# Regrouping the front of a one-core attention and MLP kernel: four max and six projection products in turn, the first maxima turned in four squares, four lead products moved behind exponential ones

## The chip, the core and the metric

The kernel runs on one core of a Trainium2 chip. The core has a matrix engine (PE, with a weight-load side PEld), a vector engine (DVE), a scalar engine (ACT), GpSimd (POOL) and a queue engine (SP) that issues transfers. PE writes into PSUM, eight banks of 128 partitions x 512 float32 numbers; DVE and ACT read them from there. The metric is device time in microseconds (us), lower is better. The kernel before took 1555.54 us, the median of three runs (1554.82 to 1555.70).

## The reference

A block of a transformer with modulated norms, 2048 rows of width 512, 32 query heads of width 16 over a single key and value head, and an MLP of width 1376:

```python
mod = (_silu(c) @ w_mod).reshape(c.shape[0], 6, 1, -1)
sa, ca, ga, sb, cb, gb = (mod[:, i] for i in range(6))
h = _layernorm(x) * (1 + ca) + sa
q, k, v = (h @ wq), h @ wk, h @ wv            # q: 32 heads of 16
p = _softmax(einsum("bhqd,bkd->bhqk", q, k) * 16 ** -0.5)
x = x + ga * (einsum("bhqk,bkd->bhqd", p, v) @ wo)
h = _layernorm(x) * (1 + cb) + sb
x = x + gb * (_gelu(h @ w1 + b1) @ w2 + b2)
```

The softmax subtracts each row's maximum, so every score is needed twice: once for the maximum, once for the exponential.

## The kernel before

**Units.** The attention is cut into 64 units: 8 blocks of 256 rows times 8 groups of four heads. For a unit there are 32 *max products* (`m`, L512: 128 query rows of one head against 512 keys, each on one half of the PE array, so two of different halves run side by side). DVE reduces each to 128 maxima (`mx`, L517). When all 32 are done, DVE reduces them again (`mm`, L565), the small result is turned, split into a high and a low part (`mh`, `ml`) and written by transfers into rows 48 and 49 of the unit's query tile `qst`. The second pass multiplies `qst` with the keys `ks` again (`e`, L617), so the result already has the maximum taken off; ACT takes the exponential (`p`, L621), and PE multiplies by the values (`acc`, L638, 16 products in a group). An `e` may only run when its unit's rows are in place.

**The loop and the front.** In the loop, each step issues four `e`, about four max products of a later unit and the `acc` group of an earlier step, with projection or MLP products between them. What stands ahead of the loop is called the front here: norms of x, turning x by PE (`tp`, L380), keys and values (`kps`, 12 products for each of four row blocks of 512, L165), the query projection (`qps`), the values' turn (`vps`, L419), the late rows of the modulation (`modl`, L297), and the first two units' 64 max products. They are taken in the order of `FIRST_MAX`: eight of unit 0 or 1 against one block of 512 keys at a time, so the first eight against key block 2 are #32 to #39, and those of unit 0 against block 3 are #40 to #47.

**What sets the order.** Every engine runs its instructions in the order in which the program issues them. In the front that order is written out by hand in the table `SLOTS`: each entry gives a number of max products and then the names of pieces of other work. `chunk(n)` issues n max products with their reductions; "keys b" and "q 1" issue three projection products at a time and, after the last, the copies out of PSUM; "low b" computes the low part of the keys on DVE (L407), which the copies on ACT must precede; "k b" copies that part to a second place by ACT (L411), where the second half of the array reads it; "v b" turns the values; "wq g" splits query weights on ACT and POOL; "rows" is a quarter of `modl`; "load" loads the query tile of unit 2. After the table the program goes on with max products until `lead[0]` = 56 are issued, then issues `keep_warm(WARM[3])`, five products into a spare bank that nobody reads (`idle`, L292), and enters the loop.

**Banks.** Max products use three banks in turn (tag `m`). Three more (`e0` to `e2`, by `ebank()`) hold the turned pieces of x, `vps`, and later the `e`. One (`x`) and one (`v`) hold `kps`, `qps`, `modl` and later `acc`. In the loop's first two steps, where no projection is under way, one max product of each step uses bank `x`.

**Placing the first maxima.** In the front, `put_max` (L545 on) runs its steps at once: DVE turns `mm` to `turned` as four 32-column squares side by side, POOL gathers them into `mt` by four copies (L560) and splits them, and four transfers (L555) write the rows: two issued on SP, two on ACT.

Of the kernel before, what the change touches and what calls it, by code (L numbers as in the profile page):

```python
# [20 lines left out]

LEAD = 6
LEAD_0 = 6
FIRST_MAX = ((0, 0), (1, 0), (0, 1), (1, 1), (0, 2), (0, 3), (1, 2), (1, 3))
SLOTS = ((2, "keys 1", "keys 1"), (2, "keys 1", "keys 1"), (2, "low 1", "heads 2"), (2, "heads 2", "k 1"), (1, "warm"), (1, "heads 2"), (2, "heads 2", "v 0"),
# [4 lines left out]
MAX_WAIT = (1, 4)  # L30
QBUFS = 4
PREP = 4
# [9 lines left out]
SOON = 6  # L42
GROUP = 4
NORM_WAIT = 6
WARM = (4, 16, 2, 5)
MOD_WAIT = 3
AHEAD = 4.5

# [1 line left out]
def raw(ap):  # L50
    return ap.bitcast(F32)
# [3 lines left out]
def adaln_mqa_mlp(  # L55
# [15 lines left out]
    nc = tc.nc  # L71
    _, S, D = x.shape
# [4 lines left out]
    BQ = 512  # L77
# [35 lines left out]
    ks = const.tile([P, S], F32R, name="ks")  # L113
# [13 lines left out]
    def ebank():  # L127
        turns[0] += 1
        return dict(tag=f"e{turns[0] % 3}", bufs=1)

    def split(dst_h, dst_l, src, eng_h, eng_l, between=None):
        if eng_h is nc.gpsimd:
            eng_h.tensor_scalar(out=dst_h, in0=src, scalar1=1.0, scalar2=0.0, op0=ALU.mult, op1=ALU.add)
# [6 lines left out]
        eng_l.tensor_tensor(out=dst_l, in0=src, in1=raw(dst_h), op=ALU.subtract)  # L140
# [19 lines left out]
    def mm3(ps, pairs, every=0, cost=0, begin=True, end=True):  # L160

        n, last = 0, 3 * len(pairs) - 1
        for wh, wl, xh, xl in pairs:
            for a, b_ in ((wh, xh), (wl, xh), (wh, xl)):
                nc.tensor.matmul(ps, a, b_, start=begin and n == 0, stop=end and n == last)  # L165
                n += 1
                if every and n % every == 0:
                    yield cost
# [50 lines left out]
    pro = pro_ctx.enter_context(tc.tile_pool(name="pro", bufs=1))  # L219
# [63 lines left out]

    idles = []

    def keep_warm(n, **place):

        for k in range(n):
            if k == 0 or not place:
                ps = psum.tile([P, BQ], F32, name=f"idle{len(idles)}", **(place or dict(tag="m", bufs=3)))  # L290
                idles.append(ps)
            nc.tensor.matmul(ps, wkH[:, 0, :], wkH.rearrange("p k n -> p (k n)"), start=True, stop=True)  # L292

    def mod_rows(ps, k, wm):

# [19 lines left out]
    wkH = pro.tile([P, KD, P], F32R, name="wkH")  # L315
# [32 lines left out]
    bigH = att.tile([P, NB - 1, KD, BQ], F32R, name="bigH", tag="bigH")  # L348
# [40 lines left out]
    kps = {}  # L389

    def kv_products(b):
        hH, hL = hts[b]
        kps[b] = psum.tile([P, BQ], F32, name=f"kps{b}", tag="x" if b == 3 else "v")
        return mm3(kps[b], [(wkH[:, k, :], wkL[:, k, :], hH[:, k, :], hL[:, k, :]) for k in range(KD)], 3)

    def kv_out(b):
        ps = kps[b]
        cols = slice(b * BQ, (b + 1) * BQ)
        vt = pro.tile([P, BQ], F32, name=f"vt{b}", tag="vt", bufs=2)
# [3 lines left out]
        vts[b] = vt  # L403

    def low_k(b):
        cols = slice(b * BQ, (b + 1) * BQ)
        nc.vector.tensor_tensor(out=ks[32:48, cols], in0=kps.pop(b)[32:48, :], in1=raw(ks[32:48, cols]), op=ALU.subtract)  # L407

    def repeat_k(b):
        cols = slice(b * BQ, (b + 1) * BQ)  # L410
        nc.scalar.copy(ks[96:112, cols], raw(ks[32:48, cols]))  # L411

    vts = {}

# [72 lines left out]
    class Max:  # L487


        def __init__(self):  # L490
# [39 lines left out]
    placed = set()  # L530
# [5 lines left out]
    def put_max(u, mx):  # L536

        T = blocks[units[u][0]][1] // P  # L540
        qst = qsts[u]
        mm = mms[u % 2]
        turned = att.tile([P, 32], F32, name=f"turned{u}", tag="turned", bufs=2)
        if u == 0:
            pad(att, 256, "pad7")  # L545
        mt = att.tile([4 * T, P], F32, name=f"mt{u}", tag="mt", bufs=2)
        mh = att.tile([4 * T, P], F32R, name=f"mh{u}", tag="mh", bufs=2)
        ml = att.tile([4 * T, P], F32R, name=f"ml{u}", tag="ml", bufs=2)

        def send():  # L550
            for s in range(2):
                for r, src in ((48, mh), (49, ml)):
                    dst = qst[64 * s + r:64 * s + r + 1].rearrange("p j (t n) -> p (j t) n", n=P)
                    ring = nc.scalar if u == 0 and s else nc.sync
                    ring.dma_start(out=raw(dst), in_=raw(src[2 * T * s:2 * T * (s + 1), :].unsqueeze(1)))  # L555
            placed.add(u)

        def gather():
            for g in range(0, P, 32):
                nc.gpsimd.tensor_scalar(out=mt[:, g:g + 32], in0=turned[g:g + 4 * T, :], scalar1=1.0, scalar2=0.0,  # L560
                                        op0=ALU.mult, op1=ALU.add)
            split(mh, ml, mt, nc.gpsimd, nc.gpsimd)

        def reduce():
            nc.vector.tensor_reduce(out=mm[:, :4 * T], in_=mx, axis=AX.X, op=ALU.max)  # L565
            nc.vector.transpose(out=turned, in_=mm)  # L566
# [669 lines left out]
    first = [sum(size[:u]) for u in range(NU + 1)]  # L1236
    mp = Max()

    def chunk(n):
# [5 lines left out]
    def k_products(b):  # L1245
        for _ in kv_products(b):
            pass

    draining[0] = True
    late = [qproj_late(b, g) for b in range(2) for g in range(KD)]  # L1250
# [10 lines left out]
    def run(job, n=99):  # L1261
        for _ in range(n):
            if next(job, True):
                return
# [30 lines left out]
    def warm():  # L1295
        keep_warm(WARM[2], tag="x")
        yield
# [17 lines left out]
    turn1(0, 3)  # L1315
    keep_warm(WARM[0])
    mod1(0, 1, pool, dve, lambda: stats1(1))
# [3 lines left out]
    rows = xhat1(1, act)  # L1321
# [8 lines left out]
    stats1(2, first_q)  # L1330
    run(rows)
    run(keys(0))
    low_k(0)
    load_mods(0)
    load_mods(1)
# [3 lines left out]
    def last_h(t):  # L1339
        if t == QT - 1:  # L1340
# [12 lines left out]
    for n, *names in SLOTS:  # L1353
        chunk(n)
        for name in names:
            next(work[name])
# [53 lines left out]
    keep_warm(WARM[3], tag="e2", bufs=1)  # L1410
# [172 lines left out]
```

## Time and profile before

| | |
|---|---|
| median of three runs | 1555.54 us (1554.82 to 1555.70) |
| the profiled execution, its own time | 1555.99 us |
| its span | 1554.1 us |
| PE busy in the span | 1537.9 us (99%) |
| DVE, ACT, POOL busy | 1398.3 (90%), 1230.4 (79%), 683.7 (44%) |
| granted PE clock | 1.00 |
| first `e` issued, start of the first `acc` group | 75.1 us, 78.9 us |

All times in the text are microseconds from the start of the span. A row of a timeline gives start, length, engine, line, operation, output and inputs, shapes and count; "x8" is a run of equal instructions merged into one row, and the brackets hold the idle time before it and what ended it. PE's products are pipelined, so the time from one start to the next says more than a row's length.

### The profile page before, as it was taken

What the parts mean: (1) busy time and instruction counts of PE and PEld (TensorE: products, weight loads), DVE (VectorE), ACT (ScalarE), POOL (GpSimd) and SP (SyncE); (2) the same over time, 40 slices, a digit from 0 to 9 for tenths busy, and PEclk for the clock granted to TensorE, in tenths of its full rate; (3) what the DMA queues carried; (4) which work ended last, traced back from release to release, by engine and by line L of the source; (5) the groups of instructions that cost most, each with busy time, mean ns of one, the idle gap of its engine ahead of it and who ended that gap; (6) DMA issues with size and microseconds to landing.
All of it is one profiled execution on the core that took longest, in us unless ns stands there. A gap on an engine that the chain in (4) does not pass through costs nothing.

```text
span 1554.1 us, 41556 instructions
## 1 busy us (share of the span) xinstructions
PE 1537.9 (99%) x16405; PEld 954.4 (61%) x16405; DVE 1398.3 (90%) x2488; ACT 1230.4 (79%) x2401; POOL 683.7 (44%) x1206
## 2 busy tenths in 40 slices
PE   7999999999999999999999999999999999999999
PEld 4455555567655665557655676556655676566658
DVE  7999999999999999999999999999999999999814
ACT  5577778788877887788877888788877888778874
POOL 5535432867422571246521563235711574046511
PEclk9999999999999999999999999999999999999999
DMA  7226412413030220303112120302212230203141
GB/s 240 102 89 199 151 57 81 130 51 97 18 105 26 72 68 28 103 19 109 33 51 79 56 87 16 111 26 88 68 30 73 60 101 25 87 28 99 48 150 48
DMA packets 84215, 120.85 MB, mean 78 GB/s; under 512 B 21342, under 2 KB 57438, under 8 KB 83764
## 3 DMA queue, kind: packets, MB, share of 16 engines
q1 hardware_dynamic: 84004, 118.18, 23.7%
q8 instruction: 130, 2.13, 0.6%
q14 instruction: 65, 0.53, 0.1%
q10 hardware_dynamic: 16, 0.00, 0.0%
HBM read 90.87 MB, written 26.74 MB: 76 GB/s over the span
## 4 chain that ended last, share of the span: by engine, by line
PE 86%; DVE 8%; issue 3%; POOL 2%; DMA 1%; ACT 0%; SPq 0%; POOLq 0%; DVEq 0%
PE acc L638 29%; PE m L512 23%; PE e L617 16%; PE w1ps L198 8%; DVE mx L517 6%; PE w2ps L198 2%; PE w2ps L188 2%; DMA xt<-in_A_x_dram 1%; PE w1ps L188 1%; PE wops L198 1%; PE tp L198 1%; PE qps L198 1%; PE kps L165 1%; DVE st L823 0%; DVE x L816 0%
## 5 line engine op out<-in xcount | busy, mean ns | idle before, releaser
L517 DVE TENSOR_REDUCE mx<-m 128x1 f32<-128x512 f32 x2048 | 1270.6, 682 | 86.6 <-PE m L512 65.1
L621 ACT ACTIVATE p<-e 128x512 f32<-128x512 f32 x2048 | 1098.8, 598 | 255.1 <-PE e L617 112.0
L512 PE MATMUL m<-ks,qst 64*128 64x512 f32 x2048 | 836.7, 429 | 2.0 <-DVE mx L517 0.6
L617 PE MATMUL e<-qst,ks 64*128 64x512 f32 x2048 | 740.2, 412 | 0.0
L638 PE MATMUL acc<-p,va 128*32 128x256 f32 x8192 | 548.0, 385 | 0.0
L512 PEld LDWEIGHTS m<-ks,qst 64*128 64x128 f32 x2048 | 368.2, 184 | 205.1 <-DVE mx L517 173.5
L617 PEld LDWEIGHTS e<-qst,ks 64*128 64x128 f32 x2048 | 359.6, 184 | 89.3 <-ACT p L621 62.5
L638 PEld LDWEIGHTS acc<-p,va 128*32 128x32 f32 x8192 | 214.0, 109 | 213.9 <-issue 110.9
L198 PE MATMUL w1ps<-h2H,w1t 64*128 64x256 f32 x1232 | 235.5, 287 | 0.0
L560 POOL TENSOR_SCALAR mt<-turned 8x32 f32<-8x32 f32 x256 | 53.1, 208 | 399.9 <-DVE turned L566 387.9
L198 PEld LDWEIGHTS w1ps<-h2H,w1t 64*128 64x128 f32 x1232 | 186.0, 185 | 28.9 <-DVE mx L517 14.8
L198 PE MATMUL w1ps<-h2L,w1t 64*128 64x256 f32 x616 | 169.3, 275 | 0.0
L198 PE MATMUL w2ps<-w2H,gH 64*128 64x512 f32 x274 | 120.3, 439 | 0.0
L198 PEld LDWEIGHTS w1ps<-h2L,w1t 64*128 64x128 f32 x616 | 114.1, 185 | 0.0
L198 PE MATMUL w2ps<-w2L,gH 64*128 64x512 f32 x274 | 107.5, 392 | 0.0
L198 PE MATMUL w2ps<-w2H,gL 64*128 64x512 f32 x274 | 106.9, 390 | 0.0
L975 POOL TENSOR_SCALAR tt<-tt 128x256 f32<-128x256 f32 x77 | 31.0, 402 | 131.5 <-ACT tt L974 96.5
L140 POOL TENSOR_TENSOR gL<-z,gH 128x256 fp32r<-128x256 f32 x77 | 57.0, 741 | 6.4
L976 POOL TENSOR_TENSOR tt<-tt,z 128x256 f32<-128x256 f32 x77 | 56.7, 736 | 6.4
L986 POOL TENSOR_TENSOR z<-tt,z 128x256 f32<-128x256 f32 x77 | 56.4, 732 | 6.0
L985 POOL TENSOR_TENSOR tt<-tt,z 128x256 f32<-128x256 f32 x77 | 56.5, 733 | 0.0
L198 PEld LDWEIGHTS w2ps<-w2H,gH 64*128 64x128 f32 x274 | 50.4, 184 | 6.7 <-DVE ot L1038 2.5
(193 smaller groups left out, 1503.5 us busy)
## 6 DMA issues: line engine op xcount, KB each, us to landing
w1t<-dw SPq DMA_DIRECT2D x82, 512.0 KB
qst<-dq SPq DMA_DIRECT2D x384, 32.0 KB
do<-oc SPq DMA_DIRECT2D x62, 128.0 KB
dw<-w1s SPq DMA_DIRECT2D x11, 512.0 KB
xt<-in_A_x_dram SPq DMA_DIRECT2D x4, 1024.0 KB
dq<-qH SPq DMA_DIRECT2D x16, 256.0 KB
dq<-qL SPq DMA_DIRECT2D x16, 256.0 KB
x<-in_A_x_dram SPq DMA_DIRECT2D x8, 512.0 KB
```

Of the source, the lines that this page charges most:

```text
L140: eng_l.tensor_tensor(out=dst_l, in0=src, in1=raw(dst_h), op=ALU.subtract)
L188: nc.tensor.matmul(ps, a, b_, start=first_, stop=last_)
L198: ins = nc.tensor.matmul(ps, a[rows], b_[rows], start=first_ and s == 0, stop=last_ and s == 1)
L512: nc.tensor.matmul(m, qsts[u][rows, j, t * P:(t + 1) * P], ks[rows, kc * 512:(kc + 1) * 512], start=True, stop=True)
L517: nc.vector.tensor_reduce(out=self.mx[u][:, i, kc:kc + 1], in_=m, axis=AX.X, op=ALU.max)
L560: nc.gpsimd.tensor_scalar(out=mt[:, g:g + 32], in0=turned[g:g + 4 * T, :], scalar1=1.0, scalar2=0.0, op0=ALU.mult, op1=ALU.add)
L617: nc.tensor.matmul(e, ks[rows, kt * P:(kt + 1) * P], rhs, start=True, stop=True)
L621: ins = nc.scalar.activation(dst, e, AF.Exp, scale=0.25)
L638: ins = nc.tensor.matmul(accs[u][32 * cidx:32 * cidx + 32, :], va[:, kt, :], rhs, start=kt == 0, stop=kt == NKT - 1)
L976: nc.gpsimd.tensor_tensor(out=tt, in0=tt, in1=z, op=ALU.mult)
L985: nc.gpsimd.tensor_tensor(out=tt, in0=tt, in1=z, op=ALU.mult)
L986: nc.gpsimd.tensor_tensor(out=z, in0=tt, in1=z, op=ALU.add)
```

## The change

Five edits, all in the front or in what opens the loop.

1. **Order.** From the twelfth entry of `SLOTS` on, four max products and six projection products stand in turn where two and three did; the value turns, the query weights 2 and 3 and the late rows have other places.
2. **Banks.** In these entries (`WIDE` to the third from the end) every second max product goes to an `e` bank instead of an `m` bank, so six banks serve the maxima.
3. **The values' copy.** `vt`, the copy of the values by ACT, is issued after the copy of the low part of the keys ("k b"), not with the other copies out of PSUM (`keep_v`).
4. **The first maxima.** For unit 0, DVE turns `mm` in four 32x32 squares straight into `mt` and splits it itself; two transfers, both issued on SP, write the rows, each one row on both halves.
5. **The lead.** `LEFT` = 4: four max products fewer are issued ahead of the loop, and the loop's first two steps take six each where they took four each. `WARM[3]` is 0: the five idle products are gone.

```diff
+LEFT = 4
 SLOTS = (... (2, "heads 3"), (2, "heads 3"), (2, "heads 3"), (2, "heads 3"),
-         (0, "keys 2"), (2, "keys 2"), (2, "keys 2"), (2, "keys 2"),
-         (2, "low 2", "k 2", "v 1", "wq 1"), (0, "keys 3"), (2, "keys 3"), (2, "keys 3"), (2, "keys 3"), (2, "low 3", "k 3"),
-         (0, "v 2"), (2, "q 1"), (2, "q 1"), (2, "q 1"),
-         (2, "q 1", "rows"), (2, "v 3", "wq 2"), (2, "rows"), (2, "rows"), (2, "rows", "wq 3", "load"))
+         (4, "keys 2", "keys 2"), (4, "keys 2", "keys 2"), (2, "low 2", 2, "k 2", "keys 3", "keys 3", "v 1", "wq 1"), (4, "keys 3", "keys 3"),
+         (2, "low 3", 2, "k 3", "wq 2", "wq 3", "q 1", "q 1"), (4, "q 1", "q 1"), (4, "v 2", "rows"),
+         (2, "v 3", "rows"), (2, "rows"), ("rows", "load"))
+WIDE = 11
-WARM = (4, 16, 2, 5)
+WARM = (4, 16, 2, 0)
...
     def kv_out(b):
...
-        nc.scalar.copy(vt[32:64, :], ps[32:64, :])
...
+    def keep_v(b):
+        vts[b] = pro.tile([P, BQ], F32, name=f"vt{b}", tag="vt", bufs=2)
+        nc.scalar.copy(vts[b][32:64, :], kps[b][32:64, :])
...
     def repeat_k(b):
         cols = slice(b * BQ, (b + 1) * BQ)
         nc.scalar.copy(ks[96:112, cols], raw(ks[32:48, cols]))
+        if b:
+            keep_v(b)
...
-                    ring = nc.scalar if u == 0 and s else nc.sync
-                    ring.dma_start(out=raw(dst), in_=raw(src[2 * T * s:2 * T * (s + 1), :].unsqueeze(1)))
+                    nc.sync.dma_start(out=raw(dst), in_=raw(src[2 * T * s:2 * T * (s + 1), :].unsqueeze(1)))
...
+        def place_first():
+            for g in range(0, P, 32):
+                nc.vector.transpose(out=mt[:, g:g + 32], in_=mm[g:g + 32, :])
+
+            def send_row(r, src):
+                dst = qst[r:r + 65:64].rearrange("p j (t n) -> p (j t) n", n=P)
+                nc.sync.dma_start(out=raw(dst), in_=raw(src.unsqueeze(1)))
+
+            split(mh, ml, mt[:4 * T], nc.vector, nc.vector, lambda: send_row(48, mh))
+            send_row(49, ml)
             placed.add(u)
...
             nc.vector.tensor_reduce(out=mm[:, :4 * T], in_=mx, axis=AX.X, op=ALU.max)
+            if u == 0:
+                place_first()
+                return
...
     def chunk(n):
         for _ in range(n):
-            mp.step(mp.done % 2)
+            mp.step(mp.done % 2, **(ebank() if wide[0] and mp.done % 2 else {}))
...
-    while mp.done < lead[0]:
+    while mp.done < lead[0] - LEFT:
         chunk(1)
```

**PE, where the order first differs** (after the last turned piece of x; `m_u_j_t_kc_s` is a max product of a unit, `kps` the keys' and values' projection of row block 2). Before:

```order
L512 MATMUL m_0_1_1_1_634<-ks,qst_157 128x512
L380 MATMUL tp_3_637<-ident,xt_151 128x128 x4
L165 MATMUL kps_646<-bigH,wkH 128x512
L165 MATMUL kps_646<-bigH,wkL 128x512
L165 MATMUL kps_646<-bigL,wkH 128x512
L512 MATMUL m_1_0_1_0_650<-ks,qst_157 128x512
L512 MATMUL m_1_0_1_1_653<-ks,qst_157 128x512
```

Now:

```order
L383 MATMUL tp_3_637<-ident,xt_151 128x128 x4
L518 MATMUL m_1_0_1_0_646<-ks,qst_157 128x512
L518 MATMUL m_1_0_1_1_649<-ks,qst_157 128x512
L518 MATMUL m_1_1_1_0_652<-ks,qst_157 128x512
L518 MATMUL m_1_1_1_1_655<-ks,qst_157 128x512
L167 MATMUL kps_658<-bigH,wkH 128x512
L167 MATMUL kps_658<-bigH,wkL 128x512
L167 MATMUL kps_658<-bigL,wkH 128x512
```

Four max products (#20 to #23) now come first, and behind the three products shown the same three follow once more before the next four max products; before, two max products stood after every three.

**PE, the end of the front and the loop's opening** (`modl` are the modulation's late rows, `e` the second pass of unit 0). Before:

```order
L297 MATMUL modl<-wml_578,csb 32x512 x4
L512 MATMUL m_1_0_2_0_879<-ks,qst_158 128x512
L512 MATMUL m_1_0_2_1_882<-ks,qst_158 128x512
L512 MATMUL m_1_1_2_0_885<-ks,qst_158 128x512
L512 MATMUL m_1_1_2_1_888<-ks,qst_158 128x512
L292 MATMUL idle_891<-wkH 128x512 x5
L617 MATMUL e_0_0_1_898<-qst_157,ks 128x512
L617 MATMUL e_0_0_0_901<-qst_157,ks 128x512
L512 MATMUL m_0_0_3_1_904<-ks,qst_158 128x512
```

Now:

```order
L300 MATMUL modl<-wml_439,csb 32x512 x4
L300 MATMUL modl<-wml_578,csb 32x512 x4
L637 MATMUL e_0_0_1_877<-qst_157,ks 128x512
L637 MATMUL e_0_0_0_880<-qst_157,ks 128x512
L518 MATMUL m_1_0_2_1_883<-ks,qst_158 128x512
L518 MATMUL m_1_0_2_0_886<-ks,qst_158 128x512
L637 MATMUL e_0_1_1_889<-qst_157,ks 128x512
L518 MATMUL m_1_1_2_0_892<-ks,qst_158 128x512
L518 MATMUL m_1_1_2_1_895<-ks,qst_158 128x512
```

The four max products #52 to #55 stood ahead of the first `e` and now stand behind it; the idle products are gone. From the first `acc` group on, PE's order is the same as before.

**DVE, the first maxima** (`mx` are the reductions of unit 0's last and unit 1's next max products). Before:

```order
L517 TENSOR_REDUCE mx_482<-m_1_1_3_0_814 128x1
L517 TENSOR_REDUCE mx_482<-m_1_1_3_1_817 128x1
L565 TENSOR_REDUCE mm_192<-mx_482 128x8
L566 STREAM_TRANSPOSE turned_820<-mm_192 128x32
L517 TENSOR_REDUCE mx_544<-m_0_0_2_0_842 128x1
```

Now:

```order
L523 TENSOR_REDUCE mx_482<-m_1_1_3_1_804 128x1
L582 TENSOR_REDUCE mm_192<-mx_482 128x8
L565 STREAM_TRANSPOSE mt_810<-mm_192 32x32 x4
L139 CAST mh_811<-mt_810 8x128
L142 TENSOR_TENSOR ml_812<-mt_810,mh_811 8x128
L523 TENSOR_REDUCE mx_544<-m_0_0_2_0_833 128x1
```

POOL's four gathering copies and its split are gone; DVE has four turns, a cast and a subtraction ahead of its next maximum.

More of the change, by code (lines that the diff above doesn't have):

```diff
@@ L284, in adaln_mqa_mlp, with keep_warm @@
     idles = []
-    def keep_warm(n, **place):
+    def keep_warm(n, src=None, **place):
+        src = wkH.rearrange("p k n -> p (k n)") if src is None else src
         for k in range(n):
@@ L291, in keep_warm @@
                 idles.append(ps)
-            nc.tensor.matmul(ps, wkH[:, 0, :], wkH.rearrange("p k n -> p (k n)"), start=True, stop=True)
+            nc.tensor.matmul(ps, src[:, :P], src, start=True, stop=True)
     def mod_rows(ps, k, wm):
@@ L398, in kv_out @@
         cols = slice(b * BQ, (b + 1) * BQ)
-        vt = pro.tile([P, BQ], F32, name=f"vt{b}", tag="vt", bufs=2)
         for r in range(2):
             nc.scalar.copy(ks[64 * r:64 * r + 48, cols], ps[64 * r:64 * r + 48, :])
-        nc.scalar.copy(vt[32:64, :], ps[32:64, :])
-        vts[b] = vt
     def low_k(b):
         cols = slice(b * BQ, (b + 1) * BQ)
-        nc.vector.tensor_tensor(out=ks[32:48, cols], in0=kps.pop(b)[32:48, :], in1=raw(ks[32:48, cols]), op=ALU.subtract)
+        nc.vector.tensor_tensor(out=ks[32:48, cols], in0=kps[b][32:48, :], in1=raw(ks[32:48, cols]), op=ALU.subtract)
+    def keep_v(b):
+        vts[b] = pro.tile([P, BQ], F32, name=f"vt{b}", tag="vt", bufs=2)
+        nc.scalar.copy(vts[b][32:64, :], kps[b][32:64, :])
     def repeat_k(b):
@@ L545, in put_max @@
             pad(att, 256, "pad7")
-        mt = att.tile([4 * T, P], F32, name=f"mt{u}", tag="mt", bufs=2)
+        mt = att.tile([4 * T if u else 32, P], F32, name=f"mt{u}", tag="mt", bufs=2)
         mh = att.tile([4 * T, P], F32R, name=f"mh{u}", tag="mh", bufs=2)
@@ L553, in send @@
                     dst = qst[64 * s + r:64 * s + r + 1].rearrange("p j (t n) -> p (j t) n", n=P)
-                    ring = nc.scalar if u == 0 and s else nc.sync
-                    ring.dma_start(out=raw(dst), in_=raw(src[2 * T * s:2 * T * (s + 1), :].unsqueeze(1)))
+                    nc.sync.dma_start(out=raw(dst), in_=raw(src[2 * T * s:2 * T * (s + 1), :].unsqueeze(1)))
+            placed.add(u)
+        def place_first():
[6 more added lines that the diff above has]
+            send_row(49, ml)
             placed.add(u)
@@ L1237, in adaln_mqa_mlp @@
     mp = Max()
+    wide = [False]
     def chunk(n):
         for _ in range(n):
-            mp.step(mp.done % 2)
+            mp.step(mp.done % 2, **(ebank() if wide[0] and mp.done % 2 else {}))
     act, dve, pool = nc.scalar, nc.vector, nc.gpsimd
-    def k_products(b):
-        for _ in kv_products(b):
-            pass
     draining[0] = True
@@ L1332, in adaln_mqa_mlp @@
     run(keys(0))
+    keep_v(0)
     low_k(0)
@@ L1352, in adaln_mqa_mlp @@
             "wq 1": one(prep_wq, 1), "wq 2": one(prep_wq, 2), "wq 3": one(prep_wq, 3)}
[L1353 to L1356, printed above, removed]
+    for i, slot in enumerate(SLOTS):
+        wide[0] = WIDE <= i < len(SLOTS) - 2
+        for part in slot:
+            if isinstance(part, int):
+                chunk(part)
+            else:
+                next(work[part])
     assert 0 in placed and len(mods_late) == KD
@@ L1408, in end_step @@
                 put_off(rest(units[u][0], units[u][0] == len(blocks) - 1))
-    keep_warm(WARM[3], tag="e2", bufs=1)
+    keep_warm(WARM[3], bigH[:, 0, 0, :], tag="v")
     behind = None
```

2 rows, old and new, of the table SLOTS are left out of this document.

## The prediction

> **What bounds the kernel now.** I read the table of windows first, then the chain of work that ended last, then each engine's timeline around the change. The windows give start:end, length, busy time of PE, PEld, DVE, ACT and POOL, granted clock, DMA share and GB/s:
>
> ```profile
> span 1554.1 us, 41556 instructions
> 47.50:60.00 12.50, 12.50 (x52) 6.47 (x51) 11.57 (x19) 7.68 (x14) 8.23 (x8) 1.00 0.00 1
> 60.00:69.50 9.50, 9.22 (x44) 3.90 (x44) 8.20 (x13) 2.89 (x8) 2.51 (x3) 1.00 0.12 45
> 75.10:81.80 6.70, 6.59 (x47) 3.49 (x46) 5.89 (x10) 5.60 (x11) 0.65 (x2) 1.00 0.10 25
> 81.80:90.40 8.60, 8.60 (x94) 5.10 (x93) 7.85 (x16) 6.51 (x12) 1.57 (x6) 1.00 0.04 11
> ```
>
> The reader is to see two engines close to full: PE has work in nearly every microsecond, VectorE (DVE) in about nine tenths. From 81.8 on PE has no gap at all. The chain says what PE's time is made of, piece by piece (start, length, what):
>
> ```profile
> 33.30 1.60 PE kps L165 x6
> 34.89 0.42 PE m L512 x2
> ...
> 46.93 0.59 PE tp L380 x4
> ...
> 48.64 0.90 PE kps L165 x3
> 49.54 0.42 PE m L512
> ...
> 52.62 0.36 PE vps L419 x4
> ...
> 69.70 1.00 PE modl L297 x8
> ...
> 73.82 1.40 PE idle L292 x5
> 75.21 0.42 PE e L617 x2
> ...
> 75.91 2.50 DVE mx L517 x4
> ...
> 78.95 1.00 PE acc L638 x16
> ...
> 81.93 1.00 PE acc L638 x16
> 84.77 1.00 PE acc L638 x16
> ```
>
> Three projection products and a pair of max products (its halves run side by side) take 0.90 + 0.42 = 1.32; six take only 1.60, because the turn between array shapes is paid once. After the first e the chain lies on DVE: "mx x4" is PE waiting for maxima to be reduced. Steps of the loop are 84.77 - 81.93 = 2.84 apart later, but the first takes 81.93 - 78.95 = 2.98. DVE's timeline (start, length, then idle time before and who ended it, in brackets):
>
> ```profile
> 43.30 4.87 DVE L517 TENSOR_REDUCE mx<-m 128x1 f32<-128x512 f32 x8 [0.16 <-PE m L512]
> 48.68 5.27 DVE L517 TENSOR_REDUCE mx<-m 128x1 f32<-128x512 f32 x8 [0.51 <-PE m L512]
> 54.04 0.68 DVE L407 TENSOR_TENSOR ks<-kps,ks 16x512 fp32r<-16x512 f32 x1
> 54.76 5.21 DVE L517 TENSOR_REDUCE mx<-m 128x1 f32<-128x512 f32 x8
> ...
> 67.05 2.48 DVE L517 TENSOR_REDUCE mx<-m 128x1 f32<-128x512 f32 x4 [1.05 <-PE m L512]
> 69.56 0.19 DVE L565 TENSOR_REDUCE mm<-mx 128x8 f32<-128x32 f32 x1
> 69.78 0.21 DVE L566 STREAM_TRANSPOSE turned<-mm 128x32 f32<-128x32 f32 x1
> 69.92 5.14 DVE L517 TENSOR_REDUCE mx<-m 128x1 f32<-128x512 f32 x8
> 75.91 7.27 DVE L517 TENSOR_REDUCE mx<-m 128x1 f32<-128x512 f32 x12 [0.85 <-PE m L512]
> ```
>
> Number the maxima of the first two units #0 to #63. A reduction that need not wait follows the last by 0.60 (12 in 7.27, 8 in 4.87); where each pair comes just in time 8 take 5.2. #19 ends at 43.30 + 4.87 = 48.17. #47, the last of unit 0, ends at 69.53. #55 ends at 75.06, and the loop's first, #56, starts at 75.91, 0.77 after e is issued (75.14 in PE's timeline, quoted below). #63 starts at 75.91 + 7 x 0.60 = **80.1**. That instant is what I follow, since from there on both kernels have the same order and PE is full.
>
> **The change part by part.** All orders are equal up to the last turn of x, which ends at 46.93 + 0.59 = 47.52.
>
> The regrouping takes 1.60 + 0.42 + about 0.23 = 2.25 on PE for four maxima, where two old groups took 2.64. The 0.23 of a second pair is the step between half-array products in the loop (PE's timeline, the last two rows here; ACT's comes first, then the e that opens the loop):
>
> ```profile
> 47.48 0.78 ACT L386 ACTIVATE h<-tp,sa,ca 128x512 f32<-128x512 f32 x1 [0.46 <-POOL bigL L140]
> 54.76 0.62 ACT L411 CAST ks<-ks 16x512 fp32r<-16x512 f32 x1 [0.75 <-DVE ks L407]
> ...
> 75.14 0.49 PE L617 MATMUL e<-qst,ks 64*128 64x512 f32 x2
> ...
> 83.20 0.39 PE L617 MATMUL e<-qst,ks 64*128 64x512 f32 x1
> 83.43 0.39 PE L512 MATMUL m<-ks,qst 64*128 64x512 f32 x1
> ```
>
> DVE needs 4 x 0.60 = 2.40 for the same four, so it, not PE, sets the pace. Followed through:
> - #20 to #22 are issued at 47.5. #23 goes into the e bank of the third turned piece, which ACT reads until 47.48 + 0.78 = 48.26. Six products follow (1.60), so #24 is ready at about 50.85; DVE did #20 to #23 by 50.5, and waits 0.35.
> - #24 to #29 end at 54.4. The low part of k (54.04 to 54.76, some 0.89 beyond a reduction's pace) ends at 55.3, and #30 and #31 at 56.5. #32 and #33 read these columns of ks: the second half only after ACT's copy (0.62), ready at 56.5, just in time.
> - #32 to #37, the next low part, ended at 61.0, then #38 to #47: #47 ends at **67.05**, 2.5 earlier than now. PE's #40 and #41 wait for that low part and its copy (61.7).
>
> Turning the first maxima moves from POOL to DVE and loses two transfers and ACT's queue. What POOL, SP and ACT do for it now, and the DMA share (next to last column) after the last issue:
>
> ```profile
> 70.08 1.02 POOL L560 TENSOR_SCALAR mt<-turned 8x32 f32<-8x32 f32 x4 [0.33 <-DVE turned L566]
> 71.19 0.29 POOL L133 TENSOR_SCALAR mh<-mt 8x128 fp32r<-8x128 f32 x1
> 71.56 0.45 POOL L140 TENSOR_TENSOR ml<-mt,mh 8x128 fp32r<-8x128 f32 x1
> ...
> 71.50 0.69 SPq L555 DMA_DIRECT2D qst<-mh  x1
> 72.29 0.61 SPq L555 DMA_DIRECT2D qst<-ml  x1
> ...
> 72.96 0.59 ACTq L555 DMA_DIRECT2D qst<-ml  x1
> ...
> 74.00:74.50 0.50, 0.50 (x3) 0.39 (x3) 0.50 (x2) 0.33 (x2) 0.41 (x1) 1.00 0.02 4
> ```
>
> On DVE: mm 0.22, four turns at the 0.14 from turned to the next start (69.78 to 69.92) 0.55, a semaphore's 0.05, and a cast and a subtraction not shown there on DVE. Their neighbours are mm's 0.19 and POOL's 0.29 and 0.45; as DVE takes 0.19 to 0.21 for small tiles I take 0.25 each. Sum 1.3, bounds 0.9 and 2.0. mh is done 1.07 after 67.05, at 68.1; SP spends 0.8 on it, so ml is issued at 68.9. Landing: ACT's last was issued at 72.96, its small movement lies in the window to 74.5, and e ran at 75.14: 1.6 to 2.2 from issue. I take 1.65, nearer the movement: **rows in place at 70.6**, 71.1 at the upper bound. DVE goes on at 68.4; #48 to #51 end at 70.8, so up to 0.9 more on DVE is hidden by its wait for e.
>
> PE on its way to e: #40 to #43 until 62.4, six products 64.0, #44 to #47 64.65, vps 0.36 and modl 1.00 to 66.0, #48 and #49 0.42, then the last vps, whose bank #47 frees at 67.05, 67.5, modl 68.5, #50 and #51 68.9, two modl 70.9. The five idle products (1.40) are gone; they only filled the wait for the rows. So **e goes at 70.9** against 75.14: 4.2 earlier, with PE and the rows within 0.3 of each other. The weight preparation that is moved forward lies in ACT's and POOL's free time (2.89 and 2.51 of 9.50 busy in the second window above) and is costed at nothing; if it held up q's low half, which SP sends ahead of the rows, e would be late by that.
>
> The four lead products: twelve maxima now follow e where eight did. #52 starts at 70.9 + 0.77 = 71.7 and #63 at 71.7 + 11 x 0.60 = 78.3. The move costs 4 x 0.60 = 2.4 of the 4.2; 1.8 is left. Then the banks: in each of the loop's first two steps one maximum goes to bank x, the others turn over three m banks. Before, #61 was the one in x, and #63 took over the bank of #59; now it is #59, and #63 takes over that of #60. So PE can issue #63 only 0.60 later than the 1.8 would allow: the first acc moves 1.2, to 77.7. With DVE ahead the first step should fall from 2.98 to 2.84, giving 0.14 back: 1.2 + 0.14 = **1.35 earlier**. Nothing later is moved, and PE stays full with DVE idle a little in each step, so this carries to the end. Bounds: if both DVE and landing are at their dear ends e goes 0.6 later (gain 0.75); if a second pair costs 0.42, not 0.23, the tail before e is 0.2 to 0.4 longer (0.4 left with both); if the bank doesn't bind, 1.95.
>
> The profiled execution took 1555.99 (its span 1554.1), 0.45 above the median 1555.54. 1555.99 - 1.35 = 1554.64; against the median **1554.2**.
>
> **The rivals.**
> - *No gap left on DVE.* From 48.17, 44 maxima at 0.60, two low parts at 0.89 and 1.3 of turning put #63's start at 48.17 - 0.68 + 26.4 + 1.8 + 1.3 = 77.0, 3.1 earlier; with the 0.14, 3.25: 1552.3. For it: the gaps of 0.51, 1.05 and 0.85 are PE's doing and PE gets lighter. Against: m waits for ACT at #23, and e comes 0.8 too late for #52.
> - *PE still paces the maxima.* If pairs come just in time as they do now (8 in 5.2), 28 maxima lose up to 28 x 0.05 = 1.4: no gain, 1555.5. For it: #32 and #40 come just in time in my own schedule.
> - *The lead is moved but e isn't early.* The four maxima cost 2.4 after e whatever the front does, so with e later than 75.14 - 2.4 = 72.75 the kernel is slower. Place: the rows. SP takes q's low half first, POOL makes that after all its weights, and both transfers and any dear DVE step come behind. e at 75.14 as now gives +2.4: 1557.9. PE would then stand from 70.9 to 75.1 without idle products. What is seen now of a standing PE is short:
>
> ```profile
> 27.61 0.66 PE L380 MATMUL tp<-ident,xt 128*128 128x128 f32 x4 [1.25 <-ACT h L386]
> ```
>
> It waited 1.25, and the granted clock is 1.00 in every window above. Were it to fall by half after a wait of 4.2, the first two acc groups of 1.00 alone would add 2.0: 1559.9, and there this rival passes +0.2%. By the Trainium skill's page "TensorE: Matmul & The Clock Gate" (section on the HAM clock gate) an idle window of about 3.4 us halves PE's clock; no run here shows such a wait, and in my forecast none comes near it.
>
> **How the numbers follow.** The forecast has 0.58 (its own range 1553.6 to 1555.1), no gap 0.17, PE pacing 0.13, late rows 0.12. 0.2% is 3.1 us here, about what a measurement of this kernel tells from no change. Only the no-gap case goes past it downwards (0.17); of the late rows some 0.07 does upwards; the rest, 0.76, is within. The range goes from the no-gap case, 1552.1, to most of the way to the late rows, 1556.8; outside are the far ends of both.
>
> **What would show it.** The group "m x4, kps x6" near 2.4 us with DVE behind it; #47 ending near 67; e near 71 and no idle products before it; DVE's twelve or more reductions in a row after e without a gap, starting 0.8 after it; the first acc near 77.7, and steps of 2.84 behind it. The forecast is wrong if e comes after 72.7, if DVE shows gaps between groups of four, or if any window after 90 us differs by more than the shift.

## The result, and the profile after

The change takes **1563.48 us** (median of 6 runs, 1563.09 to 1563.89), the kernel before 1555.76 beside it (6 runs): a ratio of 1.0048, interval 1.0035 to 1.0061. It is 7.7 us **slower**, far outside the forecast's range (1552.1 to 1556.8). The profiled execution took 1563.59, with a span of 1561.8.

The chain of work that ended last, from 59.4 to the place where the projection "q 1" goes on (start, length, what). It is the view to read first:

```profile
59.42 1.28 DVE mx L523 x2
...
60.72 0.70 DVE ks L407
...
61.44 0.61 ACT ks L415
...
62.07 0.58 ACT vt L411
...
62.67 0.42 ACT wqH L345
...
63.16 2.83 POOL wqL L346 x4
...
66.03 1.22 PE qps L167 x2
```

From 60.7 to 66.0 the end of the program hangs on the low part of the keys (DVE), then on ACT's two copies (of that part and of the values), and then on the splitting of query weights by ACT and POOL (`wqH`, `wqL`). In the kernel before, ACT stood in the chain at this place with copies of the keys and values alone, and POOL didn't at all; ACT's last piece there is

```profile
59.45 0.58 ACT vt L402
```

PE's timeline shows two groups of the new order, then who waits for these weights (brackets: idle time before, and who ended it), and at its end the opening of the loop:

```profile
50.55 0.74 PE L518 MATMUL m<-ks,qst 64*128 64x512 f32 x4
...
52.81 0.74 PE L518 MATMUL m<-ks,qst 64*128 64x512 f32 x4
...
60.12 0.39 PE L167 MATMUL qps<-h0L,wqH 128*128 128x512 f32 x1
64.06 0.58 PE L167 MATMUL qps<-h0H,wqH 128*128 128x512 f32 x1 [3.56 <-ACT wqH L345]
66.03 0.79 PE L167 MATMUL qps<-h0H,wqL 128*128 128x512 f32 x1 [1.39 <-POOL wqL L346]
...
84.72 1.90 PE L658 MATMUL acc<-p,va 128*32 128x256 f32 x16
...
89.12 1.07 PE L658 MATMUL acc<-p,va 128*32 128x256 f32 x16
...
91.96 1.07 PE L658 MATMUL acc<-p,va 128*32 128x256 f32 x16
```

Three products of "q 1" run (the row at 60.12 is the third), the fourth waits 3.56 and the fifth 1.39. The max products behind them are held up too, since PE takes its instructions in order; DVE's timeline has nothing to reduce meanwhile:

```profile
68.02 2.48 DVE L523 TENSOR_REDUCE mx<-m 128x1 f32<-128x512 f32 x4 [5.29 <-PE m L518]
...
74.24 0.19 DVE L582 TENSOR_REDUCE mm<-mx 128x8 f32<-128x32 f32 x1
74.46 0.84 DVE L565 STREAM_TRANSPOSE mt<-mm 32x32 f32<-32x32 f32 x4
75.34 0.21 DVE L139 CAST mh<-mt 8x128 fp32r<-8x128 f32 x1
75.59 0.28 DVE L142 TENSOR_TENSOR ml<-mt,mh 8x128 fp32r<-8x128 f32 x1
75.80 2.47 DVE L523 TENSOR_REDUCE mx<-m 128x1 f32<-128x512 f32 x4
```

And the windows (start:end, length, busy time of PE, PEld, DVE, ACT, POOL, granted clock, DMA share, GB/s):

```profile
60.90:64.30 3.40, 0.24 (x1) 0.19 (x1) 1.79 (x3) 2.53 (x6) 1.14 (x2) 1.00 0.00 0
64.30:67.80 3.50, 2.11 (x7) 1.00 (x6) 0.00 (x0) 0.00 (x0) 1.68 (x3) 0.51 0.00 0
67.80:71.20 3.40, 3.40 (x12) 1.83 (x8) 2.48 (x4) 0.00 (x0) 0.00 (x0) 0.51 0.00 0
...
78.00:81.40 3.40, 2.60 (x14) 1.17 (x14) 2.89 (x6) 2.19 (x5) 0.00 (x0) 1.00 0.20 48
81.40:84.80 3.40, 2.41 (x14) 0.91 (x16) 3.40 (x7) 1.94 (x4) 0.00 (x0) 1.00 0.03 10
84.80:88.20 3.40, 3.40 (x24) 1.88 (x26) 1.92 (x4) 0.99 (x2) 0.00 (x0) 0.50 0.00 0
```

PE's timeline before has the first two `acc` groups at

```profile
78.88 1.07 PE L638 MATMUL acc<-p,va 128*32 128x256 f32 x16
...
81.86 1.07 PE L638 MATMUL acc<-p,va 128*32 128x256 f32 x16
```

The granted clock, 1.00 throughout in the profiled execution before, is at half in two stretches: for 6.83 us behind the wait, and for 3.41 us from 84.8, where the loop opens. So "x16" in the first `acc` group takes 1.90 in place of 1.07, and the first step of the loop is 89.12 - 84.72 = 4.40 long, the second 2.84. The second `acc` group starts at 89.12 and not at 81.86: 7.26 later. That is nearly the whole of the 7.7.

**Which weights are waited for.** "q 1" is the projection of group 1, with weights split long before ("wq 1"). The casts that end the wait belong to "wq 2" and "wq 3", which the change put ahead of "q 1". With four row blocks k (`KD`), 512 columns (`D`) and `gs` the 128 columns of group g, the tile, what "wq g" writes, and what the projection reads are

```python
    wqH = att.tile([P, KD, D], F32R, name="wqH", tag="gH")
...
            dh = wqH[:, :, gs].rearrange("p k (a r j) -> p k a j r", j=2, r=16)[:, :, :, j, :]
...
        return [(wqH[:, k, gs], wqL[:, k, gs], hH[:, k, :], hL[:, k, :]) for k in range(KD)]
```

In memory the four k follow each other, each with the columns of all groups. What "wq 2" writes therefore reaches from its columns of k = 0 to those of k = 3, and the columns of group 1 for k = 1, 2, 3 lie between. Those for k = 0 lie ahead of it, and these are the three products that ran. A program whose waits go by such stretches and not by single columns makes the second triple wait for weights that it doesn't read. The times fit: the fourth product starts at 64.06, just behind ACT's last cast of these (four from 62.67 to 64.01), and the fifth at 66.03, just behind POOL's last subtraction (63.16 + 2.83 = 65.99).

### The profile page after: what moved, and what is told of

The parts are those of the page before. It is cut to its first block, busy times and chain, and to the rows that moved or that the text cites. A ratio compares the mean times of both kernels' runs of the same rounds, so it can differ in the third digit from the quotient of the medians.

```text
span 1561.8 us, 41535 instructions
## 1 busy us (share of the span) xinstructions
PE 1539.2 (99%) x16400; PEld 953.4 (61%) x16400; DVE 1399.1 (90%) x2493; ACT 1231.5 (79%) x2401; POOL 684.2 (44%) x1200
## 4 chain that ended last, share of the span: by engine, by line
PE 89%; DVE 8%; POOL 1%; DMA 1%; ACT 1%; issue 0%; SPq 0%; DVEq 0%; POOLq 0%
PE acc L658 31%; PE m L518 24%; PE e L637 16%; PE w1ps L200 8%; DVE mx L523 6%; PE w2ps L200 2%; PE w2ps L190 2%; PE qps L200 2%; DMA xt<-in_A_x_dram 1%; PE w1ps L190 1%; PE tp L200 1%; PE wops L200 1%; POOL xt L376 1%; DVE st L843 0%; PE kps L167 0%; DVE x L836 0%
```

## The experiments

Ahead of the regrouping, the profiled executions differ already: the reduction of maximum #19 starts between 46.81 and 48.30 us, 47.49 in the kernel before. So I give the start of the second `acc` group counted from the start of that reduction, against the same distance before (81.86 - 47.49 = 34.37), beside the medians. The last two columns are read from the one profiled execution of each kernel. Within one row the ratio is taken against the runs of the kernel before on the same chip.

| run | median, us | ratio to before, interval | 2nd `acc` group, against before | clock at half, us |
|---|---|---|---|---|
| the change | 1563.48 | 1.0048 (1.0035 to 1.0061) | +7.26 | 6.83 + 3.41 |
| wq_apart | 1557.08 | 1.0007 (0.9998 to 1.0016) | +0.36 | 3.41 |
| wq_late | 1557.10 | 1.0009 (1.0000 to 1.0018) | +1.07 | 6.83 |
| before_wq_early | 1560.95 | 1.0030 (1.0019 to 1.0041) | +5.37 | 6.83 |
| late_lead | 1557.01 | 1.0005 (0.9996 to 1.0013) | +0.21 | 3.41 |
| late_warm | 1556.62 | 0.9999 (0.9990 to 1.0007) | -1.07 | none |
| late_oldplace | 1559.50 | 1.0019 (1.0009 to 1.0028) | +3.66 | 10.24 |
| before_lead | 1562.69 | 1.0038 (1.0025 to 1.0052) | +6.12 | 13.65 |
| lead_fill | 1555.97 | 0.9995 (0.9986 to 1.0004) | -1.57 | none |
| lead_ahead | 1556.00 | 0.9997 (0.9988 to 1.0006) | -1.33 | none |
| change_fill | 1562.89 | 1.0042 (1.0028 to 1.0056) | +6.17 | 6.83 |

### Is it the weights, and is the wait a false one?

**wq_apart**: the change, with each group's weights in a stretch of their own. Nothing else is moved.

```diff
-    wqH = att.tile([P, KD, D], F32R, name="wqH", tag="gH")
+    wqH = att.tile([P, KD, KD, P], F32R, name="wqH", tag="gH")
...
-            dh = wqH[:, :, gs].rearrange("p k (a r j) -> p k a j r", j=2, r=16)[:, :, :, j, :]
+            dh = wqH[:, g].rearrange("p k (a r j) -> p k a j r", j=2, r=16)[:, :, :, j, :]
...
-        return [(wqH[:, k, gs], wqL[:, k, gs], hH[:, k, :], hL[:, k, :]) for k in range(KD)]
+        return [(wqH[:, g, k], wqL[:, g, k], hH[:, k, :], hL[:, k, :]) for k in range(KD)]
```

> The change with one edit: the split query weights lie group by group in memory (wqH[:, g, k] in place of wqH[:, k, group g]), so that the four groups are four separate ranges; every instruction stands where the change has it. Theory A (the projection's second triple waits for the casts and subtractions of groups 2 and 3, which it never reads, because their ranges interleave with its own): the waits of 3.56 and 1.39 us at 64 to 66 us vanish, the clock doesn't fall at 64, e goes near 71 and the time is 1554 to 1556 us, about 8 us below the change. Theory B (the weights' preparation itself is in the way on ACT and POOL): nothing moves by more than 1 us, about 1563. Theory C (the twelve maxima behind e and the lower clock after them are the loss): the first wait goes, but 3 us or more are kept, 1558 to 1560.

PE's timeline, the second triple and the maxima behind it:

```profile
60.94 0.40 PE L167 MATMUL qps<-h0H,wqH 128*128 128x512 f32 x1
61.18 0.40 PE L167 MATMUL qps<-h0H,wqL 128*128 128x512 f32 x1
61.41 0.39 PE L167 MATMUL qps<-h0L,wqH 128*128 128x512 f32 x1
62.06 1.38 PE L518 MATMUL m<-ks,qst 64*128 64x512 f32 x4 [0.26 <-DVE ks L407]
```

The wait is gone, with the casts and subtractions at the same place in the order: it was the layout's. The ratio falls by 0.0041, that is about 6.4 us of the 7.7. The half clock behind the wait is gone too; that of the loop's opening stays.

**wq_late**: the layout is left, and the two pieces go back behind "q 1".

```diff
-         (2, "low 3", 2, "k 3", "wq 2", "wq 3", "q 1", "q 1"), (4, "q 1", "q 1"), (4, "v 2", "rows"),
-         (2, "v 3", "rows"), (2, "rows"), ("rows", "load"))
+         (2, "low 3", 2, "k 3", "q 1", "q 1"), (4, "q 1", "q 1"), (4, "v 2", "rows"),
+         (2, "v 3", "rows", "wq 2"), (2, "rows"), ("rows", "wq 3", "load"))
```

> The change with query weights 2 and 3 prepared behind the projection again (wq 2 with the last value turn, wq 3 ahead of load), in the old layout. Theory A: as with the separate layout, 1554 to 1556 us, since the wait is gone by order instead of by place. Theory B: also 1554 to 1556, so this run alone doesn't tell A from B. Theory C: 1558 to 1560.

The same 1557.1: it may be cured by order or by layout. This run also shows the rest of the change without the wait; its timelines of PE and of DVE:

```profile
71.34 0.51 PE L637 MATMUL e<-qst,ks 64*128 64x512 f32 x2
...
78.33 1.93 PE L658 MATMUL acc<-p,va 128*32 128x256 f32 x16
...
82.89 1.07 PE L658 MATMUL acc<-p,va 128*32 128x256 f32 x16
```

```profile
67.57 0.19 DVE L582 TENSOR_REDUCE mm<-mx 128x8 f32<-128x32 f32 x1
...
68.92 0.71 DVE L142 TENSOR_TENSOR ml<-mt,mh 8x128 fp32r<-8x128 f32 x1
69.56 9.78 DVE L523 TENSOR_REDUCE mx<-m 128x1 f32<-128x512 f32 x16
```

DVE has no gap from 69.56 on, e is at 71.34, the first `acc` at 78.33 (78.88 before), and then a step of 4.56. What was won ahead of the loop is lost in its first step.

**before_wq_early**: the kernel before, with only "wq 2" and "wq 3" moved ahead of its "q 1".

```diff
-         (2, "low 2", "k 2", "v 1", "wq 1"), ... (2, "low 3", "k 3"),
+         (2, "low 2", "k 2", "v 1", "wq 1"), ... (2, "low 3", "k 3", "wq 2", "wq 3"),
...
-         (2, "q 1", "rows"), (2, "v 3", "wq 2"), (2, "rows"), (2, "rows"), (2, "rows", "wq 3", "load"))
+         (2, "q 1", "rows"), (2, "v 3"), (2, "rows"), (2, "rows"), (2, "rows", "load"))
```

> The kernel before with one edit: query weights 2 and 3 are prepared ahead of the projection of group 1, as the change has it, in the old layout. Theory A: the second triple of that projection, at 61.95 us before, waits for the last cast (about 63.1) and its second product for the last subtraction (about 65), so 3 us are lost at once, and up to 3 more if the clock falls: 1558 to 1562 us. Theory B: the same. Theory C: no loss over 1 us, since nothing else of the change is here.

PE's timeline has the same two waits:

```profile
63.23 0.51 PE L165 MATMUL qps<-h0H,wqH 128*128 128x512 f32 x1 [0.80 <-ACT wqH L342]
65.20 0.79 PE L165 MATMUL qps<-h0H,wqL 128*128 128x512 f32 x1 [1.46 <-POOL wqL L343]
```

This one move, put into the old kernel, costs 5.1 us. The waits themselves are 2.26 here, shorter than in the change, since two maxima stand between the triples. The 2.8 that are left are near what 6.83 us at half clock take from a PE that is otherwise full (3.4): a wait of some 2 us costs as much again by the clock.

### Why does the loop's opening fall to half clock?

Windows of wq_late around the opening:

```profile
71.90:75.30 3.40, 2.53 (x14) 1.03 (x13) 3.35 (x7) 2.29 (x6) 0.05 (x1) 1.00 0.17 48
75.30:78.70 3.40, 3.00 (x10) 1.25 (x14) 3.40 (x7) 1.58 (x4) 0.00 (x0) 0.50 0.00 0
```

From e on twelve maxima pace PE at DVE's 0.60 each, and PE, with less than that to do for each, stands between them: 2.53 busy of 3.40. Two ways to test it: fewer maxima behind e, and work for PE between them.

**late_lead**: wq_late, with the four maxima back ahead of e.

```diff
-LEFT = 4
+LEFT = 0
```

> wq_late with LEFT = 0: the four lead products stand ahead of the first e again, without the idle products. Theory D (what is left of the loss is the clock: twelve maxima behind e leave PE half idle for 7 us while DVE reduces them, and PE's clock is halved for the next 3.4 to 6.8 us): e comes later by two pairs, near 72.2, the opening needs eight maxima and is over within 6 us, the clock stays at 1.00, the second acc group starts near 80.4 in place of 82.9, and the time is 1554 to 1555 us, below wq_late by about 2.5. Rival E (the clock falls for lack of the idle products, whatever the lead): the clock falls between 70 and 83 as in wq_late, and the time is 1556.5 or more.

Its windows:

```profile
73.60:77.00 3.40, 3.01 (x13) 1.21 (x12) 3.40 (x6) 3.19 (x7) 0.00 (x0) 1.00 0.08 20
77.00:80.40 3.40, 3.40 (x26) 1.83 (x26) 2.58 (x5) 0.88 (x2) 0.00 (x0) 0.50 0.00 0
```

The theory that had the clock stay up is wrong as it stood. The clock fell once more, though for 3.41 instead of 6.83, behind a window with PE busy for 3.01 of 3.40. The twelve maxima make it worse, but aren't needed for it.

The profiled execution, 1555.93, is also one of the shorter of late_lead's eleven, and their granted clock, as a mean over the whole span, differs with their time: 1554.95 at 1.000, 1555.93 to 1557.01 at 0.999, 1557.87 to 1558.10 at 0.998, 1558.95 and 1558.97 at 0.997. So one and the same kernel loses from nothing to more than its profile shows, with the time that the clock stays down. The kernel before has 1.000 in all but five of its 71 executions beside these runs; those five have 0.997 to 0.999 and took 1557.40 to 1560.24.

**late_warm**: wq_late, with an idle product (its result is read by nobody) behind each of six max products of the opening. Only these are added; the maxima stay behind e.

```diff
+                if behind is None:
+                    other = [(l_, lambda f_=f_: (f_(), keep_warm(1, bigH[:, 0, 0, :], tag="v"))) for l_, f_ in other]
...
-                    other[0] = 1.0, lambda: mp.step(t, tag="x", bufs=1)
+                    other[0] = 1.0, lambda f_=keep_warm: (mp.step(t, tag="x", bufs=1), f_(1, bigH[:, 0, 0, :], tag="v") if behind is None else None)
```

> wq_late with six idle products (results unread, bank v) put between the opening's max products, one behind each of the six of one half; the lead stays behind e. Theory D: PE has 2.6 us of waiting there, so the six cost nothing, and if they keep PE busy enough the clock stays at 1.00, the second acc group starts between 80.4 and 81.0, and the time is 1554.5 to 1555.5. If six are too few, the clock falls and the time stays at 1557. Rival E says the same as D here. If neither holds (the loss isn't the clock) the clock stays up and the time stays at 1557.

Its window at the opening and, from PE's timeline, the first two `acc` groups:

```profile
75.50:78.90 3.40, 3.13 (x17) 1.29 (x19) 3.40 (x7) 2.08 (x5) 0.00 (x0) 1.00 0.00 1
```

```profile
78.73 1.07 PE L658 MATMUL acc<-p,va 128*32 128x256 f32 x16
81.58 1.07 PE L658 MATMUL acc<-p,va 128*32 128x256 f32 x16
```

The clock stays at 1.00 (1.000 as a mean in all eleven executions), and the first step is 2.85. The idle products lie in PE's waiting time: #63 starts 7.73 behind e, where it was 7.33 in wq_late, so they cost 0.4 at most, and the second `acc` group comes 2.1 earlier by the table. The median was to be 1554.5 to 1555.5; it is 1556.62, no less than that of the kernel before (1556.63), so the 1.07 by which the front is ahead here does not show in the whole time.

### What the other parts are worth

**late_oldplace**: wq_late with the old placing of the first maxima (one turn, POOL's copies and split, four transfers on two queues).

```diff
-                    nc.sync.dma_start(out=raw(dst), in_=raw(src[2 * T * s:2 * T * (s + 1), :].unsqueeze(1)))
+                    ring = nc.scalar if u == 0 and s else nc.sync
+                    ring.dma_start(out=raw(dst), in_=raw(src[2 * T * s:2 * T * (s + 1), :].unsqueeze(1)))
...
-            if u == 0:
-                place_first()
-                return
```

> wq_late with the first maxima placed as before the change (one turn on DVE, four copies and the split on POOL, four transfers, two of them issued by ACT). The forecast's reckoning: the rows land about 5 us after the maxima are reduced in place of 3.8, so e comes 1 to 2 us later than wq_late's 71.3, and with twelve maxima behind it the whole kernel with it: 1558 to 1559.5. If placing was not on the path, 1557.

PE's timeline: e waits for the last transfer.

```profile
73.06 0.59 PE L635 MATMUL e<-qst,ks 64*128 64x512 f32 x2 [2.03 <-DMA qst<-ml]
```

From the second reduction (`mm`) e comes 73.06 - 67.30 = 5.76 later, with the new placing 71.34 - 67.57 = 3.77: the new placing (four squares, split on DVE, two transfers) is worth 2.0 of e. By the two ratios it is worth 0.0010, 1.6 us, though the intervals overlap.

**before_lead**: the kernel before, with only the lead changed (four maxima behind e, no idle products).

```diff
-WARM = (4, 16, 2, 5)
+WARM = (4, 16, 2, 0)
...
-    while mp.done < lead[0]:
+    while mp.done < lead[0] - 4:
```

> The kernel before with the lead alone moved: four max products fewer ahead of the loop and no idle products. The forecast's reckoning of the lead: e can't go before the rows land near 74.6, twelve reductions follow it, so the last of the 64 starts near 82.0 in place of 80.1, 2 us later: 1557.5; and by theory D the clock falls too, for 1.5 to 2 more: 1559. If moving the lead costs nothing, 1555.8.

PE's e and the windows:

```profile
74.95 0.86 PE L617 MATMUL e<-qst,ks 64*128 64x512 f32 x2 [3.17 <-DMA qst<-ml]
```

```profile
70.50:73.90 3.40, 1.29 (x10) 0.16 (x8) 1.61 (x3) 0.57 (x2) 1.02 (x4) 1.00 0.01 2
73.90:77.40 3.50, 2.45 (x8) 1.58 (x8) 1.20 (x2) 2.20 (x5) 1.57 (x3) 0.51 0.20 52
...
80.80:84.20 3.40, 3.00 (x20) 0.94 (x19) 2.71 (x5) 0.89 (x2) 0.00 (x0) 0.50 0.00 0
84.20:87.60 3.40, 3.40 (x18) 2.14 (x14) 2.05 (x3) 1.20 (x2) 0.00 (x0) 0.50 0.00 0
```

That is the third rival by itself: the lead moved, e not early. It costs 6.1 us, more than I had set down for it, and the clock stays down for four windows: PE waits for the rows, and then, at half clock, still stands between the maxima (3.00 busy of 3.40), and the clock doesn't come back.

### Putting the parts together

**lead_fill** is late_warm with `LEFT = 0` (so four idle products in the opening), **lead_ahead** is late_lead with four idle products ahead of e (`WARM = (4, 16, 2, 4)`), and **change_fill** is the change, wait and all, with late_warm's six idle products.

```diff
-LEFT = 4
+LEFT = 0
```

> wq_late with LEFT = 0 and four idle products in the opening, one behind each max product of one half: late_lead and late_warm together. If the clock is what late_lead still lost (77.0 to 80.4 us at half speed, two steps' worth), it stays at 1.00 here, the first acc group starts near 77.3 and the second near 80.1, 1.5 us below late_lead, and the time is 1554.5 to 1555.5 beside a kernel before of 1555.5 to 1556.6: faster by 0.05 to 0.15%. If four are too few, the clock falls as in late_lead and the time is the kernel before's.

```diff
-WARM = (4, 16, 2, 0)
+WARM = (4, 16, 2, 4)
```

> wq_late with LEFT = 0 and four idle products ahead of the first e, where the kernel before has five: late_lead with them. They take about 1.1 us, but DVE has maxima until 74.7 anyway, so the last of the 64 moves by no more than 0.3 us. If the idle products of the kernel before are what kept the clock up (rival E), the clock stays at 1.00 and the second acc group starts near 80.3: 1554.5 to 1555.5. If the opening's low activity decides, the clock falls as in late_lead: 1556.5 to 1557.

```diff
+                if behind is None:
+                    other = [(l_, lambda f_=f_: (f_(), keep_warm(1, bigH[:, 0, 0, :], tag="v"))) for l_, f_ in other]
```

> The change as it is, with the six idle products of late_warm in the opening. The false wait stays, with its lower clock from 64 to 71 us; the second slow stretch, 84.8 to 88.2 us, should go. The first step of the loop then takes 2.9 us in place of 4.4, and the time is 1561.5 to 1562.5, 1 to 2 us below the change. If the two slow stretches are one effect of the wait, it stays at 1563.5.

lead_fill and lead_ahead have the clock at 1.00 throughout (1.000 as a mean in all eleven executions of each), and the front 1.6 and 1.3 us ahead of the old one; PE's timeline of lead_fill has its first `acc` groups at

```profile
77.37 1.07 PE L658 MATMUL acc<-p,va 128*32 128x256 f32 x16
...
80.22 1.07 PE L658 MATMUL acc<-p,va 128*32 128x256 f32 x16
```

Their medians are 0.5 us below that of the kernel before, with intervals that hold 1: the best versions here, and neither is shown to be faster. In the profiled executions lead_fill's lead is still 1.6 at the hundredth `acc` group (352.71 against 354.31) and 0.9 at the four hundredth (1197.88 against 1198.74). A part of that is lost in the loop: one step near 1150 us, from the 383rd `acc` group to the 384th, takes 3.2 to 3.3 us in the profiled executions of all eight kernels with the new placing, and 2.9 in all four with the old, late_oldplace among them (1156.39 - 1153.49 = 2.90, against 1154.43 - 1151.16 = 3.27 in wq_late, which differs in the placing alone). Why the placing of the first maxima should lengthen so late a step isn't shown.

change_fill has a first step of 2.84 and only the first stretch of half clock; its median is 0.6 below the change's in another set of runs, and the table's distance is 1.1 shorter. Against a wait the idle products don't help: they stand behind it.

## Why the prediction was wrong

**The step that failed.** "The weight preparation that is moved forward lies in ACT's and POOL's free time (2.89 and 2.51 of 9.50 busy in the second window above) and is costed at nothing; if it held up q's low half ... e would be late by that." The engines did have the time. But I asked only who else needs ACT and POOL, and not who reads the tile that they write. "q 1" stood behind the two pieces in the program's order and read the same tile; that it reads other columns didn't save it. The cost was 3.56 + 1.39 of standing on PE, and the clock: 0.41% of the time, 6.4 us, is gone in wq_apart, which differs in the layout alone. None of the rivals had this place. The chain's form (the weights' casts and POOL's subtractions in a stretch that had neither) was what the last part of the prediction should have named as its sign.

**The clock, a second step.** "The five idle products (1.40) are gone; they only filled the wait for the rows." They filled it with something PE needed. In the old kernel they, and four maxima ahead of e, kept PE busy for 3.12 of the 3.50 us around the first e (75.14):

```profile
72.80:76.30 3.50, 3.12 (x14) 1.64 (x13) 2.65 (x5) 1.75 (x5) 1.66 (x3) 1.00 0.12 29
```

lead_ahead shows what they were worth: it differs from late_lead in four idle products ahead of e alone, and the clock that falls in late_lead stays up.

The forecast said "the first step should fall from 2.98 to 2.84". It rose to 4.40 in the change and to 4.56 in wq_late, and is 2.85 where six idle products are added (late_warm). So the step's length was right and the clock was left out. The forecast used the half clock only for the third rival, with PE standing for 4.2 us; by the Trainium skill's page "TensorE: Matmul & The Clock Gate" (section on the HAM clock gate) the clock falls after an idle window of about 3.4 us. The windows here agree in length, but at the opening PE wasn't idle for one: with 2.41 busy of 3.40 in the change, the clock fell.

**What held**, by wq_late, where the wait is absent:

- The regrouping. A group of four maxima and six projection products was to take 2.25; in the change two of them start 52.81 - 50.55 = 2.26 apart. #47 ended at 67.5, foretold 67.05.
- The placing. 1.3 on DVE, bounds 0.9 and 2.0; it took 75.80 - 74.24 = 1.56 in the change and 69.56 - 67.57 = 1.99 in wq_late. The term was 0.3 to 0.7 too small: the four turns took 0.21 each in place of 0.14, and in wq_late the subtraction 0.71 in place of 0.25. The 0.05 for a semaphore had no row; between these rows of the change lie 0.03 to 0.04. No e waited for the rows in either.
- e at 71.34, foretold 70.9; #63 7.33 behind it, foretold 7.4; the first `acc` at 78.33, foretold 77.7.
- The size of the gain at the loop's opening, though not at the end. 1.35 earlier at the second `acc` group: 1.07 with the clock held (late_warm), 1.57 with the lead put back as well (lead_fill). The move of the lead, then, brought nothing that these runs show; what they show is the regrouping and the placing. But "Nothing later is moved ... so this carries to the end" did not hold: at the end of the span, counted as in the table, late_warm is 0.50 ahead of the kernel before and lead_fill 0.25, and their medians are 0.0 and 0.5 below its own. The step near 1150 us takes 0.4 of that; the rest is open.

So the 7.7 us are the false wait with its half clock (about 6.4, shown by wq_apart), and about 1.2 that are left without it (wq_apart and wq_late; their intervals just hold 1): the half clock of the opening, which eats the front's gain, and what is lost behind it.

**The third rival** was right as a mechanism and too cheap: alone it costs 6.1 (before_lead) and not 2.4 or 4.4, as four windows at half clock were not in its sum.

## What to carry to other kernels

Before work is moved ahead "into free time", list every later reader of the tiles that it writes, and take for written the whole stretch from the first to the last byte: groups that are prepared one by one belong in stretches of their own. A product that nobody reads may still be doing something, so ask of each piece of filler what the clock does without it. Where a change makes one engine the pace of another, count the busy time of the waiting PE per window of about 3.4 us, not only its longest wait.

## What the runs showed of the hardware

- **Half clock comes in whole windows.** All stretches here are 3.41, 6.83, 10.24 or 13.65 us long: one to four times 3.41. One in which PE is partly idle can be followed by one at half speed, and here the clock came back only behind a window with PE busy throughout: 3.00 of 3.40 at half clock (wq_late, before_lead) was followed by more of it. What share decides isn't settled, and busy time alone doesn't decide: 2.41, 2.53 and even 3.01 busy of 3.40 were followed by half clock, 2.60 of 3.40 in the change (78.00 to 81.40) wasn't, nor was 2.14 of 3.42 in the kernel before (25.13 to 28.55, with full-array products). Whether the half-array products that make up most of the opening count for less was not tried.
- **A small subtraction beside POOL.** `ml` (8x128) took 0.28 on DVE in the change, with POOL free, and 0.71 in wq_late, where POOL was in a run of weight subtractions of 2.96 / 4 = 0.74 each, as POOL's timeline of wq_late has it:

```profile
68.69 2.96 POOL L346 TENSOR_TENSOR wqL<-wqf,wqH 128x256 fp32r<-128x256 f32 x4 [1.42 <-ACT wqH L345]
```

  By the Trainium skill's page "SBUF — State Buffer" (section on the two separate sides) a DVE operation with two inputs in that memory and a POOL operation that reads it exclude each other for a whole instruction. By the row POOL's run began at 68.69, so its first operation ended near 69.43; the subtraction, issued at 68.92, ended at 69.63, which agrees. It took 0.71 or 0.72 in all five kernels that split these weights late with the new placing, and 0.28 in the three that split them early.
